# Another written order for all of the attention stage of a hash-attention, mixture and spatial-gating kernel

## The chip, the cores and the metric

The kernel runs on one core of one Trainium2 chip. The metric is the device time of one execution in microseconds (us), the median of three runs. The engines are named as the profile names them: PE is TensorE's matmul, PEld its weight load, DVE is VectorE, ACT is ScalarE, POOL is GpSimd, SP is SyncE, which here only issues DMAs.

## What is computed

Three layers stand one behind the other. The first is attention whose mask is a hash: every query and every key gets six sign bits from a projection, and a query sees the keys with the same bits. The other two are token mixers made of matrix products.

```python
def _attn_ref(q, k, v, proj):            # q, k, v: (2, 8, 768, 64)
    q_bucket, k_bucket = ...             # six sign bits of q @ proj, k @ proj
    mask = q_bucket[:, :, :, None] == k_bucket[:, :, None, :]
    scores = np.where(mask, scale * np.matmul(q, k.transpose(0, 1, 3, 2)), -1000000000.0)
    attn = np.exp(scores - np.max(scores, axis=-1, keepdims=True))
    attn = attn / (np.sum(attn, axis=-1, keepdims=True) + 1e-09)
    return np.matmul(attn, v)

def reference(**kwargs):
    x = attention output, reshaped to (2, 768, 512)
    x = _moe_ref(x)       # k = relu(xk @ w_k); v = k*k @ w_v; r = sigmoid(xr @ w_r); r * v
    return _moe2_ref(x)   # relu(x @ w_in), normalise one half, mix over tokens, gate, @ w_out
```

## The kernel before

**The attention stage.** Two heads form a pair, and there are eight pairs. A pair has two groups (halves of its 768 queries), and a group has six units: two heads times three blocks of 128 queries. So there are 96 units and 16 groups. Nothing decides the order of the work at run time. A table of words in `attention()`, the string `order`, is read word by word, and each word records a few instructions on fixed engines. Each engine then carries out its own instructions in just that order and waits by semaphores for the others. A letter is a step, and the number behind it is the unit, the group, the pair, or the half unit:

- `S` (scores, L395) is four products of 384 columns on PE into one of two score banks of PSUM; the next unit but one needs the same bank again.
- `K` (peak, L405) is DVE's pass over the scores of a unit (scaling, and the row's extreme); it frees the score bank.
- `X` (expo, L417) is the exponential on ACT.
- `T` (group, L427) is three PE transposes of half a unit into one of three PSUM banks. `E` and `V` (evac, L433) copy such a bank into the tile PT: `E` on ACT, `V` on DVE. Every half unit has one of the two, 192 in all.
- `A` (av, L462) is the value products of half a group: six products of 384 columns, which the profile records as twelve matmuls, into one bank, `obank`. Two `A` make a group. `F` (finish, L474) is DVE's multiplication of that bank by the reciprocal sums; the next group's first `A` needs the bank free and so waits for `F`.
- `R` (recip, L442 to L448) is the reciprocal of a group's sums: three short DVE instructions, then four DMAs from SP; `D` (spread) sends the result back as a broadcast that `F` reads.
- `Z` (bits_mm, L293) is the projection of the next pair on PE, eight short matmuls in the profile, into one of the three transpose banks; `G` turns it into signs on DVE (L300) and scales it on POOL (L311). `P` and `B` place these bits by DMA.
- `x`, `v`, `L` are loads; `Q` (L276) splits rows on POOL; `W` with two numbers is step by step the preparation of the first mixer's weights: L42 and L72 on ACT, L45, L50, L56, L63 and L66 on DVE, L77 and L78 on POOL.
- `M`, `N`, `b`, `e`, `p`, `s` are the first work of the next stage (mixing tokens on DVE, ACT and POOL, and gate products of PE), `t` and `Y` set its plan going.

From unit 24 to unit 60 the table repeats itself every 12 units (one pair); before and behind it is irregular.

**The mixers** follow in `mixers()`, whose order comes from a plan of ticks that the change leaves alone. Their matrix products run on PE to the end.

Of the kernel before, what the change touches and what calls it, by code (L numbers as in the profile page):

```python
# [233 lines left out]
def attention(tc, nc, mid, wide, top, dram, ident, msc, omu, misc, cst_sb, pb, epsT, kq, vP, XT, TK0, wr, w_r, wk,
              w_k, w_v, ps_s, ps_t, obank, mix_jobs, r_products, r_sigmoid, tick, now, at_tick, plan_weight, wv, **_):
    PS = bass.MemoryType.PSUM
    with ExitStack() as ctx:
# [340 lines left out]
        order = """
S0 S1 w3 K0 S2 K1 X0 T0 X1 l1 T1 T2 K2 E0 S3 E1 E2 T3 K3 X2 S4 W0.0 Z1 V3 W1.0 X3 T5 K4 T4 E5 X4 G1 S5 T7 E4 T6 E7
K5 S6 T8 S7 K6 X5 T9 R0 E6 E8 X6 T11 S8 V9 Q1.0 T10 T12 K7 Q1.2 E11 T13 S9 Q1.1 E10 W0.1 K8 W0.2 X7 A0 X8 E12 Q1.3  # L580
E13 K9 W0.3 W0.4 Q1.6 D0 T15 T14 T16 E15 X9 S10 P0 Q1.7 E14 Q1.5 K10 S11 E16 T17 K11 W0.5 T18 X10 E18 T19 E19 S12
V17 W1.1 K12 S13 X11 W0.6 T20 E20 P1 T21 v1 A1 T22 Q1.4 E21 T23 S14 X12 W0.7 K13 E22 T25 T24 E23 W1.2 F0 x2 S15 K14
R1 S16 W1.3 X13 K15 T27 X14 A2 E24 L2 W1.4 V25 E27 Z2 W1.6 G2 T29 T28 X15 S17 Q2.3 Q2.2 Q2.0 E29 W1.7 E28 T26 E26
K16 A3 T30 Q2.6 K17 Q2.1 T31 Q2.5 X16 Q2.7 Q2.4 X17 W2.0 E30 S18 E31 T35 K18 T32 T33 V33 S19 E35 E32 T34 X18 S20 T37
K19 T36 B2 E34 X19 E36 K20 S21 T39 V37 K21 S22 V39 T38 V38 X20 X21 T40 E40 S23 T41 E41 T43 T42 E43 K22 D1 S24 W3.0
K23 X22 S25 X23 x3 W0.8 T45 R2 T44 W1.5 F1 A4 A5 R3 W2.1 E44 V45 E42 K24 X24 W2.2 K25 W1.8 L3 W2.3 W3.1 T47 T46 S26
Z3 W2.4 E47 E46 T48 W2.5 W2.6 W2.7 T49 S27 X25 G3 E48 Q3.2 Q3.0 K26 T51 D2 Q3.3 X26 E49 Q3.6 Q3.4 Q3.7 T50 S28 K27
E51 W3.2 S29 F2 X27 W3.3 K28 W3.4 T52 T53 A6 K29 A7 X28 E50 v2 X29 W3.6 E52 W3.7 T54 Q3.5 T55 V53 Q3.1 W4.0 E54 S30
E55 T59 K30 T56 T57 V57 S31 E59 E56 T58 X30 S32 T61 K31 T60 B3 E58 X31 E60 K32 S33 T63 V61 K33 S34 V63 T62 V62 X32
X33 T64 E64 S35 T65 E65 T67 T66 E67 K34 D3 S36 W5.0 K35 X34 S37 X35 x4 W2.8 T69 R4 T68 W3.5 F3 A8 A9 R5 W4.1 E68 V69  # L590
E66 K36 X36 W4.2 K37 W3.8 L4 W4.3 W5.1 T71 T70 S38 Z4 W4.4 E71 E70 T72 W4.5 W4.6 W4.7 T73 S39 X37 G4 E72 Q4.2 Q4.0
K38 T75 D4 Q4.3 X38 E73 Q4.6 Q4.4 Q4.7 T74 S40 K39 E75 W5.2 S41 F4 X39 W5.3 K40 W5.4 T76 T77 A10 K41 A11 X40 E74 v3
X41 W5.6 E76 W5.7 T78 Q4.5 T79 V77 Q4.1 W6.0 E78 S42 E79 T83 K42 T80 T81 V81 S43 E83 E80 T82 X42 S44 T85 K43 T84 B4
E82 X43 E84 K44 S45 T87 V85 K45 S46 V87 T86 V86 X44 X45 T88 E88 S47 T89 E89 T91 T90 E91 K46 D5 S48 W7.0 K47 X46 S49
X47 x5 W4.8 T93 R6 T92 W5.5 F5 A12 A13 R7 W6.1 E92 V93 E90 K48 X48 W6.2 K49 W5.8 L5 W6.3 W7.1 T95 T94 S50 Z5 W6.4
E95 E94 T96 W6.5 W6.6 W6.7 T97 S51 X49 G5 E96 Q5.2 Q5.0 K50 T99 D6 Q5.3 X50 E97 Q5.6 Q5.4 Q5.7 T98 S52 K51 E99 W7.2
S53 F6 X51 W7.3 K52 W7.4 T100 T101 A14 K53 A15 X52 E98 v4 X53 W7.6 E100 W7.7 T102 Q5.5 T103 V101 Q5.1 W8.0 E102 S54
E103 T107 K54 T104 T105 V105 S55 E107 E104 T106 X54 S56 T109 K55 T108 B5 E106 X55 E108 K56 S57 T111 V109 K57 S58
V111 T110 V110 X56 X57 T112 E112 S59 T113 E113 T115 T114 E115 K58 D7 S60 W9.0 K59 X58 S61 X59 x6 W6.8 T117 R8 T116
W7.5 F7 A16 A17 R9 W8.1 E116 V117 E114 K60 X60 W8.2 K61 W7.8 L6 W8.3 W9.1 T119 T118 S62 Z6 W8.4 E119 E118 T120 W8.5  # L600
W8.6 W8.7 T121 S63 X61 G6 E120 Q6.2 Q6.0 K62 T123 D8 Q6.3 X62 E121 Q6.6 Q6.4 Q6.7 T122 S64 K63 E123 W9.2 S65 F8 X63
W9.3 K64 W9.4 T124 T125 A18 K65 A19 X64 E122 v5 X65 W9.6 E124 W9.7 T126 Q6.5 T127 V125 Q6.1 W10.0 S66 B6 E126 E127
K66 T129 E129 T128 E128 S67 x7 W8.8 T131 K67 X66 T130 S68 V131 E130 T133 X67 S69 D9 E133 T132 E132 K68 T135 T134 K69
X68 V135 F9 X69 S70 S71 T137 K70 R10 T136 V136 A20 K71 E134 W10.1 W10.2 E137 T138 X70 T139 X71 L7 E138 T141 S72 E139
S73 M0 D10 E141 T140 T143 R11 E140 K72 X72 T142 K73 S74 E143 M1 K74 Z7 A21 E142 M2 T144 T145 W10.3 G7 S75 W10.4 X73
V144 T146 X74 T147 E145 W11.0 E146 T148 W9.5 K75 S76 S77 T149 X75 V147 Q7.4 K76 E148 T151 X76 E149 K77 Q7.0 T150 X77
F10 Q7.6 S78 V151 S79 D11 Q7.3 K78 T152 T153 V150 v6 E152 A22 A23 X78 T154 V153 W9.8 T155 B7 E155 K79 R12 v7 V154
S80 X79 Q7.1 K80 Q7.2 T157 E157 T156 S81 V156 T158 T159 Q7.7 X80 K81 S82 E158 S83 X81 E159 K82 N0 T161 T160 E161 K83
S84 T163 V160 F11 T162 W10.6 X82 M3 E163 S85 T164 T165 E162 K84 X83 A24 Q7.5 W11.1 X84 A25 W10.5 T166 W10.7 N1 E164
D12 K85 R13 N2 V165 T167 N3 V166 S86 S87 T169 X85 K86 E167 T168 W10.8 E169 T170 F12 X86 S88 E168 T171 A26 K87 K88  # L610
X87 M4 E170 T174 E171 T173 M5 T172 X88 S89 M6 V174 S90 W12.0 T175 K89 E172 E173 K90 N4 N5 X89 W12.1 D13 T177 T176
E177 E176 V175 S91 K91 S92 T178 T179 W11.2 K92 X90 E179 X91 A27 X92 T180 E180 V178 N6 W11.3 T183 S93 M7 R14 S94
W11.4 E183 T182 T181 N7 F13 A28 V182 D14 K93 b0 A29 E181 K94 X93 T184 b1 e0 W11.6 X94 T188 S95 T187 E188 V184 T185
E187 T186 W12.2 b2 W11.5 E186 K95 p0 F14 e1 E185 X95 T190 E190 R15 Y t T189 T191 b3 e2 e3 E191 W11.7 D15 t b4 E189
W12.3 A30 A31 t W11.8 p1 b5 W12.4 W12.6 W12.7 t F15 s0 t s1 t b6
"""
# [573 lines left out]
```

## Time and profile before

| what | value |
|---|---|
| median of three runs | 526.62 us (526.17 to 526.82) |
| the profiled execution | 526.15 us |
| span of its instructions | 524.3 us |
| PE, DVE, ACT, POOL busy in it | 518.0, 417.9, 331.1, 149.3 us |
| evictions L433 on ACT and on DVE | 146 and 46 |

The times in the rows count from the span's start. A row of the timeline has the start, the duration, the engine, the line, the operation, what it writes and reads, sizes and how many instructions were merged into the row; in brackets stands idle time of the engine ahead of it and what ended it. The durations of matmuls are modelled and overlap (a product begins before the one ahead of it is through), so what a block of products costs PE is read as the distance from its start to the start of the next block.

### The profile page before, as it was taken

How to read it: one execution, taken by the hardware profiler on the slowest of the kernel's cores; microseconds unless marked ns; L12 is line 12 of the kernel's file. 1: busy time of each engine (PE TensorE's matmuls, PEld its weight loads, DVE VectorE, ACT ScalarE, POOL GpSimd, SP SyncE). 2: the span in 40 equal slices, each digit the busy share in tenths (PEclk: the TensorE clock that was granted, in tenths of full speed). 3: DMA queues.
4: the chain of work that ended last, by engine and by line, in shares of the span. 5: the costliest groups of instructions: out<-in, count | busy, mean ns of one | idle time of the engine just before them, and what ended most of it. 6: DMA issues, size and time to landing. Idle time of an engine off the chain costs nothing.

```text
span 524.3 us, 8289 instructions
## 1 busy us (share of the span) xinstructions
PE 518.0 (99%) x2850; PEld 417.0 (80%) x2850; DVE 417.9 (80%) x849; ACT 331.1 (63%) x682; POOL 149.3 (28%) x159
## 2 busy tenths in 40 slices
...
GB/s 231 192 210 153 179 191 139 179 170 180 160 164 147 89 71 17 92 5 41 80 41 80 42 67 54 81 40 55 73 126 60 61 45 5 43 7 114 1 20 102
DMA packets 20042, 49.88 MB, mean 95 GB/s; under 512 B 3776, under 2 KB 7424, under 8 KB 20000
## 3 DMA queue, kind: packets, MB, share of 16 engines
...
q10 hardware_dynamic: 432, 0.28, 0.2%
q14 instruction: 19, 0.16, 0.1%
...
## 4 chain that ended last, share of the span: by engine, by line
PE 94%; DVE 4%; ACT 1%; issue 1%; DVEq 0%
PE o L183 13%; PE v L700 12%; PE o L462 12%; PE t L427 11%; PE s L395 11%; PE k L183 9%; PE s L183 7%; PE r L183 6%; PE u L183 5%; PE w L183 5%; DVE p L405 2%; PE z L293 1%; DVE tk L380 1%; DVE rc L442 0%; DVE PT L433 0%
## 5 line engine op out<-in xcount | busy, mean ns | idle before, releaser
L405 DVE TENSOR_SCALAR_CACHE_REDUCE p<-s 128x768 f32<-128x768 f32 x96 | 91.1, 953 | 16.0 <-PE s L395 12.5
L417 ACT ACTIVATE p<-p,m 128x768 f32<-128x768 f32 x96 | 90.1, 940 | 12.9 <-DVE p L405 12.2
L395 PE MATMUL s<-tk 128*128 128x384 f32 x384 | 86.9, 356 | 0.6 <-DVE tk L336 0.4
L131 POOL TENSOR_TENSOR tk<-g,tk 128x384 fp32r<-128x384 f32 x8 | 9.0, 1141 | 270.5 <-PE s L183 233.5
L427 PEld LDWEIGHTS t<-ident,p 128*128 128x128 f32 x576 | 65.8, 140 | 18.6 <-ACT p L417 4.9
L427 PE MATMUL t<-ident,p 128*128 128x128 f32 x576 | 79.8, 275 | 0.2 <-ACT p L417 0.2
L433 ACT COPY PT<-t 128x384 f32<-128x384 f32 x146 | 64.7, 476 | 23.2 <-PE t L427 23.0
L700 PE MATMUL v<-k,wv 128*128 128x512 f32 x288 | 68.8, 389 | 0.0
L462 PE MATMUL o<-PT,v 128*64 128x384 f32 x384 | 66.3, 491 | 0.9 <-DVE XT L474 0.9
L395 PEld LDWEIGHTS s<-tk 128*128 128x128 f32 x384 | 62.6, 189 | 3.2 <-POOL tk L341 0.9
L700 PEld LDWEIGHTS v<-k,wv 128*128 128x128 f32 x288 | 54.1, 188 | 11.2
L276 POOL TENSOR_TENSOR tk<-x,tk 64x384 fp32r<-64x384 f32 x56 | 59.3, 1079 | 10.2 <-DMA tk<-in_kq_dram 9.0
L462 PEld LDWEIGHTS o<-PT,v 128*64 128x64 f32 x384 | 25.8, 136 | 32.1 <-issue 30.4
L686 DVE TENSOR_TENSOR k<-kt,k 128x512 fp32r<-128x512 f32 x24 | 16.6, 690 | 24.8 <-ACT k L685 24.7
L183 PE MATMUL k<-tk,wk 128*128 128x512 f32 x144 | 35.6, 389 | 0.0
L183 PEld LDWEIGHTS k<-tk,wk 128*128 128x128 f32 x144 | 27.0, 188 | 5.6
L130 ACT CAST tk<-g 128x384 fp32r<-128x384 f32 x16 | 8.2, 513 | 36.2 <-DVE g L966 36.2
L156 DVE SCALAR_TENSOR_TENSOR f<-XT,msc,d 128x256 f32<-128x256 f32 x48 | 24.1, 503 | 6.5 <-ACT d L150 5.1
L433 DVE COPY PT<-t 128x384 f32<-128x384 f32 x46 | 24.7, 547 | 2.1 <-PE t L427 2.0
L183 PE MATMUL r<-tk,wr 128*128 128x512 f32 x108 | 25.7, 391 | 0.0
L66 DVE SCALAR_TENSOR_TENSOR w_a<-w_raw,w_p 128x512 f32<-128x512 uint32 x32 | 24.2, 755 | 1.0
L42 ACT ACTIVATE w_a<-w_raw 128x512 f32<-128x512 f32 x32 | 21.7, 678 | 4.7 <-DMA w_raw<-in_w_in_dram 3.7
(188 smaller groups left out, 934.4 us busy)
## 6 DMA issues: line engine op xcount, KB each, us to landing
...
```

The source lines that it names most:

```text
L42: nc.scalar.activation(st["a"].bitcast(F32), st["raw"][:, :, 1].bitcast(F32), AF.Abs)
L66: nc.vector.scalar_tensor_tensor(st["a"].bitcast(F32), st["raw"][:, :, 0], 2.0 ** -52, st["p"].bitcast(F32), op0=ALU.mult, op1=ALU.mult,)
L156: nc.vector.scalar_tensor_tensor(st["f"], x, mu, st["d"], op0=ALU.mult, op1=ALU.add)
L183: nc.tensor.matmul(o, a, x, start=(i == 0), stop=(i == len(seq) - 1))
L276: nc.gpsimd.tensor_sub(tk[l, 1 + 2 * t, o], raw[pp][l, t, o], tk[l, 2 * t, o])
L395: nc.tensor.matmul(s[:, c, :HS], w, t[:, n, c * HS:(c + 1) * HS], start=(n == 0), stop=(n == 1),)
L405: nc.vector.tensor_scalar(c, s[:, :, :HS], -0.125, BIG / 16, op0=ALU.mult, op1=ALU.min, accum_out=m)
L417: nc.scalar.activation(c, c, AF.Exp, bias=m, scale=-1.0, accum_out=den[g][:, u:u + 1])
L427: nc.tensor.transpose(t[:, 128 * n:128 * n + 128], p[:, k0:k0 + 128], ident)
L433: copy(PT[g][:, e, 3 * c:3 * c + 3, 128 * j:128 * j + 128], t[:, :HS].rearrange("p (n q) -> p n q", n=3),)
L462: nc.tensor.matmul(obank[64 * e:64 * e + 64, :HS], vt[g // 2][:, kt, e, :], PT[g][:, e, kt, :], start=(kt == 0), stop=(kt == 5),)
L700: nc.tensor.matmul(o, w, x, start=(c == 0 and k == 0), stop=(c == 7 and k == 2))
```

## The change

It replaces the string `order` and nothing else. Both strings hold 1004 words, and each engine does the same kinds of work. 61 half units are evicted by DVE (`V`) in the new string and 131 by ACT, where it was 46 and 146. The value products stand in 19 uninterrupted runs instead of 20, and six of the seven projections `Z` stand directly ahead of or behind a run of value products, where it was two.

```diff
-X47 x5 W4.8 T93 R6 T92 W5.5 F5 A12 A13 R7 W6.1 E92 V93 E90 K48 X48 W6.2 K49 W5.8 L5 W6.3 W7.1 T95 T94 S50 Z5 W6.4
...
+W5.5 K47 S48 V89 S49 F5 T92 D6 T93 W6.1 W5.8 E92 V93 A12 X47 W7.1 K48 L5 A13 K49 W6.2 W6.3 R7 W7.2 E90 Z5 W6.4 W7.3
```

**PE at the head of a pair, before** (units 36 to 38; `z` is the projection, `o` the value products, `t` transposes, `s` scores):

```order
L395 MATMUL s<-tk_0_84 128x384 x8
L427 MATMUL t<-ident,p 128x128 x6
L462 MATMUL o_76<-PT,v 64x384 x12
L427 MATMUL t<-ident,p 128x128 x6
L395 MATMUL s<-tk_0_84 128x384 x4
L293 MATMUL z<-x,msc 32x384 x4
L427 MATMUL t<-ident,p 128x128 x6
L395 MATMUL s<-tk_1_85 128x384 x4
```

The same place on PE with the change:

```order
L395 MATMUL s<-tk_0_84 128x384 x8
L427 MATMUL t<-ident,p 128x128 x6
L462 MATMUL o_76<-PT,v 64x384 x12
L293 MATMUL z<-x,msc 32x384 x4
L427 MATMUL t<-ident,p 128x128 x3
L395 MATMUL s<-tk_0_84 128x384 x4
L427 MATMUL t<-ident,p 128x128 x6
```

The projection moved from between scores and transposes to directly behind the value products.

**DVE from the end of one pair to the head of the next, before** (`p` is the pass over the scores, `rc` the reciprocal, `XT` the finish, `PT` an eviction):

```order
L405 TENSOR_SCALAR p,m<-s 128x768 x2
L442 TENSOR_SCALAR rc_95<-den 128x6
L443 RECIPROCAL rc_95<-rc_95 128x6
L445 STREAM_TRANSPOSE rt<-rc_95 128x32
L474 TENSOR_TENSOR XT<-o_76,rb 128x384
L442 TENSOR_SCALAR rc_96<-den 128x6
L443 RECIPROCAL rc_96<-rc_96 128x6
L445 STREAM_TRANSPOSE rt<-rc_96 128x32
L433 COPY PT<-t 128x3x128
L405 TENSOR_SCALAR p,m<-s 128x768
```

The same place on DVE with the change:

```order
L405 TENSOR_SCALAR p,m<-s 128x768
L442 TENSOR_SCALAR rc_95<-den 128x6
L443 RECIPROCAL rc_95<-rc_95 128x6
L445 STREAM_TRANSPOSE rt<-rc_95 128x32
L405 TENSOR_SCALAR p,m<-s 128x768 x2
L433 COPY PT<-t 128x3x128
L474 TENSOR_TENSOR XT<-o_76,rb 128x384
L433 COPY PT<-t 128x3x128
L405 TENSOR_SCALAR p,m<-s 128x768 x2
```

The first reciprocal moved from directly ahead of the finish to two score passes and one eviction ahead of it; the second moved behind (it is six rows further on). An eviction now stands ahead of the finish and another behind it.

## Rows read from the trace of the kernel before

**Rows 1.** The page: busy time, share of the span, instructions of three engines.

```profile
PE 518.0 (99%) x2850; PEld 417.0 (80%) x2850; DVE 417.9 (80%) x849; ACT 331.1 (63%) x682; POOL 149.3 (28%) x159
```

**Rows 2.** The page: the chain that ended last, by engine.

```profile
PE 94%; DVE 4%; ACT 1%; issue 1%; DVEq 0%
```

**Rows 3.** Waits of PE, 16 to 222 us: total us, times, longest.

```profile
PE o L462 <- DVE XT L474: 0.9, 2, 0.5
```

**Rows 4.** Timeline of PE, about a projection between scores and transposes.

```profile
110.14 0.94 PE L395 MATMUL s<-tk 128*128 128x384 f32 x4
111.01 0.85 PE L293 MATMUL z<-x,msc 128*32 128x384 f32 x8
111.79 0.87 PE L427 MATMUL t<-ident,p 128*128 128x128 f32 x6
112.42 0.94 PE L395 MATMUL s<-tk 128*128 128x384 f32 x4
113.21 0.82 PE L427 MATMUL t<-ident,p 128*128 128x128 f32 x6
113.78 1.70 PE L395 MATMUL s<-tk 128*128 128x384 f32 x8
```

**Rows 5.** Timeline of PE, a projection that directly follows value products.

```profile
37.27 0.85 PE L293 MATMUL z<-x,msc 128*32 128x384 f32 x8
38.05 0.87 PE L427 MATMUL t<-ident,p 128*128 128x128 f32 x6
```

**Rows 6.** Timeline of PE, a short and a long run of value products.

```profile
198.81 2.16 PE L462 MATMUL o<-PT,v 128*64 128x384 f32 x12
200.90 0.88 PE L427 MATMUL t<-ident,p 128*128 128x128 f32 x6
201.53 1.66 PE L395 MATMUL s<-tk 128*128 128x384 f32 x8
203.03 0.82 PE L427 MATMUL t<-ident,p 128*128 128x128 f32 x6
203.77 4.09 PE L462 MATMUL o<-PT,v 128*64 128x384 f32 x24
207.79 0.88 PE L427 MATMUL t<-ident,p 128*128 128x128 f32 x6
```

**Rows 7.** Timeline of all engines, the first of the two waits of PE.

```profile
51.24 1.31 POOL L78 TENSOR_TENSOR wr<-w_b,w_a 128x512 fp32r<-128x512 f32 x1
...
51.38 1.20 DVE L442 TENSOR_SCALAR rc<-den 128x6 f32<-128x6 f32 x1
...
52.97 0.52 DVE L474 TENSOR_TENSOR XT<-o,rb 128x384 f32<-128x384 f32 x1
...
53.54 0.87 PE L462 MATMUL o<-PT,v 128*64 128x384 f32 x4 [0.39 <-DVE XT L474]
```

**Rows 8.** One line's instructions: duration in ns, shortest, median, longest.

```profile
L442 DVE TENSOR_SCALAR rc<-den x16: 159/170/1265, 18.4 to 212.8; 128x6 f32<-128x6 f32 x16
```

**Rows 9.** Timeline, one unit from its scores to its second transposes.

```profile
44.28 0.94 PE L395 MATMUL s<-tk 128*128 128x384 f32 x4
...
45.35 0.96 DVE L405 TENSOR_SCALAR_CACHE_REDUCE p<-s 128x768 f32<-128x768 f32 x1 [0.23 <-PE s L395]
...
46.34 0.94 ACT L417 ACTIVATE p<-p,m 128x768 f32<-128x768 f32 x1 [0.28 <-DVE p L405]
...
47.44 0.54 PE L427 MATMUL t<-ident,p 128*128 128x128 f32 x3
```

**Rows 10.** Windows of one pair each: length, then busy us of PE, PEld, DVE, ACT, POOL.

```profile
50.00:76.00 26.00, 25.61 (x177) 18.90 (x176) 24.49 (x50) 20.95 (x47) 20.84 (x20) 1.00 0.79 197
76.00:102.00 26.00, 26.00 (x181) 19.29 (x180) 22.48 (x50) 21.57 (x47) 15.90 (x17) 1.00 0.67 150
```

**Rows 11.** Timeline of DVE: two evictions and the pass behind them.

```profile
126.74 1.02 DVE L433 COPY PT<-t 128x384 f32<-128x384 f32 x2
127.68 0.95 DVE L405 TENSOR_SCALAR_CACHE_REDUCE p<-s 128x768 f32<-128x768 f32 x1
```

More of the change, by code (lines that the diff above doesn't have):

```diff
@@ L578, in attention @@
         order = """
[L579 to L593, printed above, removed]
@@ L594, in attention @@
-E82 X43 E84 K44 S45 T87 V85 K45 S46 V87 T86 V86 X44 X45 T88 E88 S47 T89 E89 T91 T90 E91 K46 D5 S48 W7.0 K47 X46 S49
-X47 x5 W4.8 T93 R6 T92 W5.5 F5 A12 A13 R7 W6.1 E92 V93 E90 K48 X48 W6.2 K49 W5.8 L5 W6.3 W7.1 T95 T94 S50 Z5 W6.4
-E95 E94 T96 W6.5 W6.6 W6.7 T97 S51 X49 G5 E96 Q5.2 Q5.0 K50 T99 D6 Q5.3 X50 E97 Q5.6 Q5.4 Q5.7 T98 S52 K51 E99 W7.2
-S53 F6 X51 W7.3 K52 W7.4 T100 T101 A14 K53 A15 X52 E98 v4 X53 W7.6 E100 W7.7 T102 Q5.5 T103 V101 Q5.1 W8.0 E102 S54
-E103 T107 K54 T104 T105 V105 S55 E107 E104 T106 X54 S56 T109 K55 T108 B5 E106 X55 E108 K56 S57 T111 V109 K57 S58
@@ L599, in attention @@
[L599 to L613, printed above, removed]
@@ L614, in attention @@
-E187 T186 W12.2 b2 W11.5 E186 K95 p0 F14 e1 E185 X95 T190 E190 R15 Y t T189 T191 b3 e2 e3 E191 W11.7 D15 t b4 E189
-W12.3 A30 A31 t W11.8 p1 b5 W12.4 W12.6 W12.7 t F15 s0 t s1 t b6
+S0 S1 w3 K0 S2 K1 X0 T0 l1 X1 T1 T2 K2 E0 S3 E1 V2 K3 T3 X2 E3 S4 W0.0 Z1 K4 T5 G1 S5 T4 X3 T7 X4 W1.0 E4 T6 E7 V5
+S6 E6 K5 K6 P0 X5 T9 T8 S7 E9 v1 T10 T11 X6 S8 V8 R0 Q1.2 T12 K7 Q1.1 E10 W0.1 E11 T13 X7 K8 W0.2 S9 E12 W1.1 S10 X8
+T14 E13 T15 K9 V14 X9 K10 W0.3 Q1.3 P1 E15 A0 T16 T19 E16 X10 T17 E17 S11 Q1.0 V19 S12 T18 T20 K11 K12 Q1.4 T21 X11
@@ new lines, in attention @@
+E18 E20 Q1.6 S13 S14 X12 Q1.7 T23 T22 W0.4 E22 E21 K13 K14 X13 W0.6 A1 R1 E23 T25 T27 Q1.5 W1.2 W1.3 T24 E25 W0.7
+S15 X14 V27 S16 E24 T26 T28 T29 K15 x2 D0 L2 V26 X15 K16 F0 S17 Z2 G2 W1.4 Q2.3 V28 W1.6 Q2.0 K17 W1.7 X16 A2 Q2.1
+Q2.2 V29 A3 W0.5 T31 Q2.5 T30 Q2.6 Q2.7 X17 Q2.4 W2.0 E31 S18 T32 V30 T33 E32 K18 E33 S19 X18 T34 T35 S20 K19 E34 B2
+V35 X19 T37 T36 S21 E37 K20 W3.0 T39 V36 X20 D1 T38 K21 R2 E39 x3 E38 X21 S22 T40 K22 E40 W0.8 T41 S23 T43 E43 X22
+T42 W1.5 K23 S24 V41 S25 F1 T44 D2 T45 W2.1 W1.8 E44 V45 A4 X23 W3.1 K24 L3 A5 K25 W2.2 W2.3 R3 W3.2 E42 Z3 W2.4
@@ new lines, in attention @@
+W3.3 X24 T47 S26 G3 W2.5 Q3.3 T46 T49 X25 W2.6 E47 v2 S27 Q3.1 T48 E49 V46 Q3.5 K26 X26 E48 T51 T50 K27 S28 F2 Q3.7
+E50 V51 S29 Q3.0 T52 Q3.4 T53 Q3.2 W2.7 Q3.6 A6 W3.4 V52 X27 A7 K28 X28 W3.6 E53 K29 T55 W3.7 X29 T54 W4.0 E55 S30
+T56 V54 T57 E56 K30 E57 S31 X30 T58 T59 S32 K31 E58 B3 V59 X31 T61 T60 S33 E61 K32 W5.0 T63 V60 X32 D3 T62 K33 R4
+E63 x4 E62 X33 S34 T64 K34 E64 W2.8 T65 S35 T67 E67 X34 T66 W3.5 K35 S36 V65 S37 F3 T68 D4 T69 W4.1 W3.8 E68 V69 A8
+X35 W5.1 K36 L4 A9 K37 W4.2 W4.3 R5 W5.2 E66 Z4 W4.4 W5.3 X36 T71 S38 G4 W4.5 Q4.3 T70 T73 X37 W4.6 E71 v3 S39 Q4.1
@@ new lines, in attention @@
+T72 E73 V70 Q4.5 K38 X38 E72 T75 T74 K39 S40 F4 Q4.7 E74 V75 S41 Q4.0 T76 Q4.4 T77 Q4.2 W4.7 Q4.6 A10 W5.4 V76 X39
+A11 K40 X40 W5.6 E77 K41 T79 W5.7 X41 T78 W6.0 E79 S42 T80 V78 T81 E80 K42 E81 S43 X42 T82 T83 S44 K43 E82 B4 V83
+X43 T85 T84 S45 E85 K44 W7.0 T87 V84 X44 D5 T86 K45 R6 E87 x5 E86 X45 S46 T88 K46 E88 W4.8 T89 S47 T91 E91 X46 T90
+W5.5 K47 S48 V89 S49 F5 T92 D6 T93 W6.1 W5.8 E92 V93 A12 X47 W7.1 K48 L5 A13 K49 W6.2 W6.3 R7 W7.2 E90 Z5 W6.4 W7.3
+X48 T95 S50 G5 W6.5 Q5.3 T94 T97 X49 W6.6 E95 v4 S51 Q5.1 T96 E97 V94 Q5.5 K50 X50 E96 T99 T98 K51 S52 F6 Q5.7 E98
@@ new lines, in attention @@
+V99 S53 Q5.0 T100 Q5.4 T101 Q5.2 W6.7 Q5.6 A14 W7.4 V100 X51 A15 K52 X52 W7.6 E101 K53 T103 W7.7 X53 T102 W8.0 E103
+S54 T104 V102 T105 E104 K54 E105 S55 X54 T106 T107 S56 K55 E106 B5 V107 X55 T109 T108 S57 E109 K56 W9.0 T111 V108
+X56 D7 T110 K57 R8 E111 x6 E110 X57 S58 T112 K58 E112 W6.8 T113 S59 T115 E115 X58 T114 W7.5 K59 S60 V113 S61 F7 T116
+D8 T117 W8.1 W7.8 E116 V117 A16 X59 W9.1 K60 L6 A17 K61 W8.2 W8.3 R9 W9.2 E114 Z6 W8.4 W9.3 X60 T119 S62 G6 W8.5
+Q6.3 T118 T121 X61 W8.6 E119 v5 S63 Q6.1 T120 E121 V118 Q6.5 K62 X62 E120 T123 T122 K63 S64 F8 Q6.7 E122 V123 S65
@@ new lines, in attention @@
+Q6.0 T124 Q6.4 T125 Q6.2 W8.7 Q6.6 A18 W9.4 V124 X63 A19 K64 X64 W9.6 E125 K65 T127 W9.7 X65 T126 W10.0 B6 D9 V127
+S66 T128 W8.8 E128 V126 T129 E129 K66 S67 R10 T130 K67 T131 X66 S68 T132 E130 X67 K68 T133 S69 S70 V133 E131 E132
+X68 T134 K69 E134 X69 T135 S71 E135 W11.0 K70 x7 T136 W9.5 F9 T137 S72 L7 X70 V136 T139 T138 A20 K71 A21 E137 X71
+W10.1 V138 T140 V139 T141 K72 W10.2 E140 v6 T142 E141 R11 M0 W10.3 S73 D10 T143 X72 S74 M1 K73 E142 V143 Q7.2 K74
+F10 T144 T145 S75 Z7 X73 X74 E144 E145 W10.4 K75 G7 W10.5 W9.8 X75 M2 A22 T146 T147 S76 E147 T151 E151 V146 T149 K76
```

9 lines of the change are left out of this document (added).

## Prediction

> **What bounds the kernel now.** I read the page's first part first: PE is busy 518.0 us of the span, DVE 417.9 and ACT 331.1 [rows 1]. Then the chain that ended last: 94% of it is PE [rows 2]. A busy PE can still hide waits, so the third view is PE's own list of waits inside the attention stage. From 16 to 222 us it has one line: value products that waited for DVE's finish, twice, 0.9 us in all [rows 3]. So PE paces the attention stage almost without a gap. A new order can win in two ways only: PE's own products become cheaper by their neighbours, or these 0.9 us go. It can lose in one way: PE waits where it did not. That 15 evictions go from ACT to DVE wins nothing by itself, since nobody waited for ACT; it spends DVE's slack.
>
> **PE's own time: the projections.** The cost of a block is the distance between the starts of blocks. A projection between scores and transposes takes 0.78 us (111.01 to 111.79). But its neighbours pay too: the four score products ahead of it last 0.87 (110.14 to 111.01), where ahead of transposes they last 0.79 (112.42 to 113.21), and the six transposes behind it 0.63 (111.79 to 112.42) instead of 0.57 (113.21 to 113.78) [rows 4]. That is 0.08 + 0.06 = 0.14 us. Directly behind value products a projection takes 0.78 as well (37.27 to 38.05) [rows 5], and the value products' own neighbours have paid already [rows 6]. So each of the four projections more that stand beside value products saves 0.14: 4 x 0.14 = 0.56 us.
>
> **PE's own time: one run less.** A run of 12 recorded products takes 2.09 us (198.81 to 200.90), one of 24 takes 4.02 (203.77 to 207.79) [rows 6]; two short ones are 4.18, so joining saves 0.16. The transposes ahead of a run take 0.74 (203.03 to 203.77) instead of 0.57, of which the scores get 0.08 back that they pay behind transposes: in a double block of scores (1.50 us, 201.53 to 203.03) the second four cost 0.71 instead of 0.79 [rows 4, 6]. The transposes behind a run take 0.63 instead of 0.57. So one run less saves 0.16 + 0.09 + 0.06 = 0.31, and both edits 0.87 us. This needs no free engine and no luck. I take it whole.
>
> **The waits for the finish.** At 51.38 us the first instruction of a reciprocal takes 1.20 us; it ends as POOL's addition (51.24, 1.31 long) ends [rows 7]. The same instruction has a median of 0.17 us over its 16 places, and 1.27 at its longest [rows 8]. The reciprocal stands directly ahead of the finish in DVE's queue, so the finish starts only at 52.97, and the value products at 53.54, after 0.39 us of idle PE [rows 7]. The Trainium skill explains this kind of row (SBUF — State Buffer, "Who interferes with whom"): some DVE instructions need the port pair that GpSimd also uses, and whichever comes second blocks until the other is through. By the same section an instruction with a PSUM source, as these evictions are, does not take part; no row here shows the reverse.
>
> In the new order that reciprocal stands two score passes and one eviction earlier, the other one stands behind the finish, and the finish is recorded before the transposes that precede the value products. What is late next on DVE is then an eviction and two passes, with their own slack (below). So I count the 0.9 us [rows 3] as gone.
>
> **What the new order adds: work for DVE.** Two evictions in a row and the next pass start 0.94 us apart [rows 11], 0.47 each. Fifteen more are 7 us of DVE over the stage; in each repeated pair it is 8 evictions instead of 6, so 0.94 us. They lie beside PE's work as long as DVE has room. DVE was busy 24.49 of 26 us in one pair and 22.48 in the next, with 50 instructions in both [rows 10]; the 2.0 us between them is what blocked instructions cost. After the change that would be 25.4 and 23.4. There is room, but little in a pair with blocked instructions. ACT gets lighter, which is worth nothing here.
>
> **What it adds: the reciprocal among the passes.** The chain of a unit is in one place of the trace without company: scores start at 44.28, the pass at 45.35 (1.07 later), the exponential at 46.34, the transposes at 47.44 [rows 9]. At the end of a pair the new order alternates four scores and six transposes (0.79 + 0.57 = 1.36 us). Scores of unit i+2 need the bank of unit i, so the pass has 2 x 1.36 = 2.72 us from the start of its scores, and needs 1.07 + 0.96 = 2.03: 0.69 to spare. The transposes of unit i come 2 x 1.36 + 0.79 = 3.51 behind the scores and need 3.16: 0.35 to spare. Into this the reciprocal is now put, between two passes. Its whole length on DVE is 1.59 us where its first instruction was blocked (51.38 to 52.97) [rows 7], so 0.56 unblocked. The pass ahead of it ends 2.03 behind its own scores, the reciprocal 2.59, that is 1.23 behind the scores of the next unit: its pass is 0.16 late, which the spare time covers. Blocked by another 1.1, it is 1.26 late, and PE waits 1.26 - 0.69 = 0.57 us. Four pairs end so: between 0 and 2.3 us. POOL is busy 15.90 to 20.84 of 26 us [rows 10], so the instruction often meets one; but it then waits for the rest of it, on average half of 1.3 us, which the spare time nearly covers. I take 0.15 a pair, 0.6 us in all, nearer to the lower end since that is what the slack of the rows gives.
>
> Elsewhere (the irregular first 24 and last 36 units) I found passes with the same 2.72 us or less between scores that share a bank, as before, and cost the difference at nothing, with 0.5 us to either side for the range. At the very end a gate product moves ahead of the last value products; the mixing steps on DVE behind the last finish become fewer, so I cost it at nothing too. The same loads stand in the order, and PE waits for none of them inside the stage [rows 3].
>
> **Sum.** 526.15 (the profiled execution) - 0.87 - 0.9 + 0.6 = 524.98. The median of the runs lies 0.47 above that execution, so 525.45, stated as 525.4.
>
> **Rivals.**
> - *The waits come back elsewhere.* The port conflict is not removed, only put ahead of other work. If in two to four pairs the reciprocal is fully blocked, PE loses 1.1 to 2.3 us in place of 0.6. For it: POOL does the same work as before. Against it: in the trace only two blocked instructions reached PE at all [rows 3], although the difference of the two pairs is 2.0 us each [rows 10]. Time: 526.62 - 1.77 + 1.1 to 2.3 = 526.0 to 527.2.
> - *DVE becomes the bound, slower.* With 0.94 us more a pair it needs 25.4 of 26 us in a pair with blocked instructions. From one blocked instruction more (1.1 us) it no longer fits: 26.5, so 0.5 us a pair; with two more, 1.6 a pair. Over four pairs 2.0 to 6.4 us, so 526.8 to 531.2, in the middle 529. For it: rows 10 and the spare 0.35 us ahead of transposes. Against it: an eviction has no strict due time except through three banks, and the other pairs had 3.5 us idle. The Trainium skill speaks on this side (Perfetto Trace Analysis, "Optimizing Scalar/DVE Operations"): where DVE is saturated, work goes from it to Scalar, and the change moves it the other way. By the page the sum would come out in this rival; by the busy share of 80% [rows 1] DVE isn't saturated.
> - *The order does not do what it says.* Excluded for PE: the order of the built program shows the projections beside the value products.
>
> **How the numbers follow.** The forecast (new waits between 0 and 0.9, so 524.3 with 0.5 gained elsewhere, to 525.9) gets 0.52, the returning waits 0.36, the DVE bound 0.12. A measurement of this kernel can tell about 0.2%, 1.05 us, from no change; that puts the line for faster at 525.57. Of the forecast 0.46 lies below it, and 0.02 of the second case if the start also gains: 0.48 faster, 0.40 within, 0.12 slower. The range goes from 524.3, nothing new and 0.4 gained, to 527.4, all four reciprocals blocked and 0.3 lost elsewhere; some 0.07 is left out below and 0.13 above.
>
> **What would show it.** Right: projections with 0.78 us behind value products and no 0.87 ahead of them; 19 runs, the long ones 4.02; no wait of PE for the finish; the next stage's products starting 1 to 1.5 us earlier than before. Wrong: scores waiting for the pass (PE for DVE L405) more than 1 us in all, with a long L442 ahead; transposes waiting for ACT or for a bank; DVE above 25 us in 26. The forecast falls if these sum to more than 1.8 us.

## The result, and the profile after

The change is slower: 531.28 us (529.70 to 533.40, six runs) against 526.00 (525.58 to 526.82, six runs) of the kernel before in the same comparison, a ratio of 1.0096 with an interval of 1.0071 to 1.0121. The profiled execution took 530.67 us with a span of 528.0, where before it was 526.15 and 524.3. So 3.7 us of its loss lie inside the span, and some 0.8 us around it.

The page after: busy time (as [rows 1]), then the chain that ended last (as [rows 2]).

```profile
PE 518.5 (98%) x2850; PEld 417.6 (79%) x2850; DVE 422.7 (80%) x864; ACT 325.1 (62%) x667; POOL 150.2 (28%) x159
...
PE 88%; DMA 4%; DVE 3%; ACT 2%; POOL 2%; issue 1%; SPq 1%; POOLq 0%; DVEq 0%; ACTq 0%
```

PE is as busy as before. But the chain has 88% of PE where it had 94%, and 4% of DMA where it had none. PE's list of waits says where the time is; it is the view of [rows 3], same stretch, total us, times, longest:

```profile
PE o L462 <- DVE XT L474: 3.6, 3, 2.5
PE s L395 <- DVE p L405: 0.7, 1, 0.7
PE t L427 <- DVE zb L300: 0.4, 1, 0.4
```

That is 4.7 us of waits instead of 0.9. The line that was to go, value products waiting for the finish, has grown from 0.9 to 3.6. The third line lies at the start of the stage:

```profile
16.33 0.92 PE L427 MATMUL t<-ident,p 128*128 128x128 f32 x6 [0.38 <-DVE zb L300]
```

Transposes wait there for DVE's sign step of a projection (L300).

**The finish waits for its broadcast.** Timeline of the longest wait, rows of DVE, PE and of SP's queue (SPq):

```profile
160.31 1.29 SPq L448 DMA_DIRECT2D ds<-rt  x4
161.71 1.09 SPq L455 DMA_DIRECT2D rb<-ds  x2
...
167.78 0.56 DVE L474 TENSOR_TENSOR XT<-o,rb 128x384 f32<-128x384 f32 x1 [2.58 <-DMA rb<-ds]
...
168.39 2.16 PE L462 MATMUL o<-PT,v 128*64 128x384 f32 x12 [2.47 <-DVE XT L474]
```

The same broadcast and finish in the kernel before:

```profile
162.08 1.20 SPq L455 DMA_DIRECT2D rb<-ds  x2
...
168.62 0.55 DVE L474 TENSOR_TENSOR XT<-o,rb 128x384 f32<-128x384 f32 x1
```

DVE stood idle for 2.58 us ahead of the finish `F10` until a DMA, the broadcast `rb<-ds` of the reciprocal sums (`D10`), had landed. In SP's queue that broadcast stands behind the four DMAs of the twelfth reciprocal `R11`, whose DVE part is done only at 160.3. The table of before has `D10` ahead of `R11`; the new one has it behind. The broadcast isn't issued later than before (161.71 against 162.08). But the new order wants it earlier: DVE was ready for `F10` at 165.20, where before the finish came at 168.62, 3.1 us after the broadcast was complete (165.55 in the trace).

At two ends of pairs the finish waits in the same way. SP's queue of the change there, then the chain of work, then the same place of the queue before:

```profile
122.51 0.44 SPq L38 DMA_DIRECT2D w_raw<-in_w_k_dram  x1
123.00 1.15 SPq L455 DMA_DIRECT2D rb<-ds  x2
```
```profile
123.54 7.32 DMA rb<-ds
130.86 0.02 issue
130.88 0.57 DVE XT L474
```
```profile
122.59 1.13 SPq L455 DMA_DIRECT2D rb<-ds  x2
123.83 0.51 SPq L38 DMA_DIRECT2D w_raw<-in_w_k_dram  x1
```

A weight load of 512 KB (`W9.0`) now stands ahead of the broadcast (two DMAs of 96 KB), where it stood behind it. By the traces the broadcast was complete 7.9 us after its issue (123.00 to 130.86), before 3.4 us (122.59 to 125.96). Its second DMA took 7.32 us to land and the value products lost 0.68 us: 1.42 from the transposes' start at 130.08 to theirs at 131.50, where transposes ahead of value products take 0.74 [rows 6].

**A reciprocal among the passes was blocked.** DVE, and the scores of PE behind it:

```profile
148.68 1.50 DVE L442 TENSOR_SCALAR rc<-den 128x6 f32<-128x6 f32 x1
```
```profile
150.08 0.82 PE L427 MATMUL t<-ident,p 128*128 128x128 f32 x6
151.55 1.84 PE L395 MATMUL s<-tk 128*128 128x384 f32 x8 [0.65 <-DVE p L405]
```

From 150.08 to 151.55 are 1.47 us for transposes that cost 0.57 [rows 4]: 0.90 lost, and the double block of scores behind takes 0.18 more than in [rows 6]. The blocked instruction ends as POOL's L77 (148.86, 1.29 long) ends. It is longer than that one because it already met the tail of the POOL instruction ahead (L276, 147.89 to 148.91). It belongs to `R10`, which lies behind unit 60, where the table no longer repeats. At the ends of the four repeated pairs (`R2`, `R4`, `R6`, `R8`) the same instruction took 0.39, 0.32, 0.17 and 0.69 us, and PE waited for no pass there.

**PE's own products did become cheaper.** Timeline of PE:

```profile
131.50 4.09 PE L462 MATMUL o<-PT,v 128*64 128x384 f32 x24 [0.60 <-DVE XT L474]
135.52 0.85 PE L293 MATMUL z<-x,msc 128*32 128x384 f32 x8
136.30 0.55 PE L427 MATMUL t<-ident,p 128*128 128x128 f32 x3
...
137.97 0.94 PE L395 MATMUL s<-tk 128*128 128x384 f32 x4
138.75 1.14 PE L427 MATMUL t<-ident,p 128*128 128x128 f32 x9
```

The long run costs 4.02 (131.50 to 135.52), the projection behind it 0.78, and the scores 0.78, as [rows 4 to 6] price them. With such prices put on every block of the stage, its blocks sum to 0.95 us less than before (an estimate), and the time over the prices grows by 4.65: the difference is the 3.7 us of the span.

### The profile page after: what moved, and what is told of

Read it like the earlier page. It is cut to its first block, busy times and chain, and to the rows that moved or that the text cites. A ratio compares the mean times of both kernels' runs of the same rounds, so it can differ in the third digit from the quotient of the medians.

```text
span 528.0 us, 8278 instructions
## 1 busy us (share of the span) xinstructions
PE 518.5 (98%) x2850; PEld 417.6 (79%) x2850; DVE 422.7 (80%) x864; ACT 325.1 (62%) x667; POOL 150.2 (28%) x159
## 3 DMA queue, kind: packets, MB, share of 16 engines
HBM read 45.11 MB, written 3.19 MB: 91 GB/s over the span
## 4 chain that ended last, share of the span: by engine, by line
PE 88%; DMA 4%; DVE 3%; ACT 2%; POOL 2%; issue 1%; SPq 1%; POOLq 0%; DVEq 0%; ACTq 0%
PE o L183 13%; PE v L700 12%; PE o L462 11%; PE k L183 9%; PE t L427 9%; PE s L395 8%; PE s L183 7%; PE r L183 6%; PE u L183 5%; PE w L183 5%; DMA rb<-ds 4%; PE z L293 1%; ACT p L417 1%; DVE p L405 1%; POOL tk L336 1%
## 5 line engine op out<-in xcount | busy, mean ns | idle before, releaser
L427 PE MATMUL t<-ident,p 128*128 128x128 f32 x576 | 80.2, 275 | 0.6 <-DVE zb L300 0.4
L427 PEld LDWEIGHTS t<-ident,p 128*128 128x128 f32 x576 | 66.5, 140 | 16.6 <-issue 7.3
L433 ACT COPY PT<-t 128x384 f32<-128x384 f32 x131 | 58.9, 473 | 16.1 <-PE t L427 15.8
L276 POOL TENSOR_TENSOR tk<-x,tk 64x384 fp32r<-64x384 f32 x56 | 59.9, 1084 | 12.0 <-DMA tk<-in_kq_dram 10.0
L433 DVE COPY PT<-t 128x384 f32<-128x384 f32 x61 | 33.4, 551 | 7.8 <-PE t L427 7.8
L56 DVE SCALAR_TENSOR_TENSOR w_b<-w_raw,w_a 128x512 uint32<-128x512 uint32 x32 | 23.6, 738 | 0.7
```

Of the source, the lines that this page charges most:

```text
L56: nc.vector.scalar_tensor_tensor(st["b"], st["raw"][:, :, 1], 0xC0000000, st["a"], op0=ALU.bitwise_and, op1=ALU.bitwise_or,)
L276: nc.gpsimd.tensor_sub(tk[l, 1 + 2 * t, o], raw[pp][l, t, o], tk[l, 2 * t, o])
L427: nc.tensor.transpose(t[:, 128 * n:128 * n + 128], p[:, k0:k0 + 128], ident)
L433: copy(PT[g][:, e, 3 * c:3 * c + 3, 128 * j:128 * j + 128], t[:, :HS].rearrange("p (n q) -> p n q", n=3),)
```

## The experiments

Each diff is of the table of words, cut to the words that move; where several places change alike, it shows the first of them. The theory at first: broadcasts come late by what stands ahead of them in SP's queue (A). The rivals: DVE is too full (B), and what each expectation names. "Before" is always the kernel before on the same chip in the same comparison; it had a median between 525.76 and 526.35.

**One cause each, and both.** `e1_spread_ahead` moves `D10`, `e2_loads_behind` the four weight loads, `e3_both` both.

```diff
-E141 R11 M0 W10.3 S73 D10 T143
+E141 D10 R11 M0 W10.3 S73 T143
```
```diff
-K20 W3.0 T39 V36 X20 D1 T38
+K20 T39 V36 X20 D1 W3.0 T38
```

> The changed order with one word moved: D10 (the broadcast of group 10's sums) stands ahead of R11 instead of two scores behind it, so that its DMA no longer stands behind R11's four DMAs in SP's queue. Theory A (the broadcast lands late): the finish of group 10, which waited 2.58 us for the broadcast, waits 0 to 0.3, and the time falls by about 2.5 us, to 528.8. Theory B (DVE is the bound, because of 15 more evictions): PE then waits for a score pass or a bank instead; less than 0.5 us comes back.

> The changed order with four weight loads (W3.0, W5.0, W7.0, W9.0; 512 KB each) recorded directly behind the broadcasts D1, D3, D5, D7 instead of directly or shortly ahead of them, as in the kernel before. Theory A: the broadcast takes less than the 7.3 us seen behind a load, the two waits of the value products at 78 and 130 us (0.60 and 0.68 us beyond the block's usual time) go, 1.2 us less, 530.0. Theory B: no change beyond 0.3 us.

> Both of the edits to the changed order. Theory A: 3.7 us less than the changed kernel, 527.5; PE waits for no finish. What is left over the kernel before must then be a blocked reciprocal among the score passes (0.9 us at 150 us) and the start (0.5 us at 15 us), less 0.9 us of cheaper products. Theory B: 531, with waits for passes and banks.

Measured, here and below as median, ratio to the kernel before and its interval: 530.30 (1.0090, 1.0061 to 1.0119); 530.89 (1.0102, 1.0079 to 1.0126); 526.92 (1.0024, 1.0004 to 1.0043). Alone they bring next to nothing, together more than 4 us. The queue's order is the main cause, but the two places don't add up. A part of that is PE's clock, which can fall behind a long wait (below): three of the four runs of `e2_loads_behind` show a mean granted clock of 0.994 to 0.997, nine of the ten of `e3_both` 0.999 or 1.000. With `D10` ahead the finish is still waited for three times, 2.5 us in all, the longest (1.8) at the end of a pair; with the loads behind, the one wait at `F10` stays:

```profile
PE o L462 <- DVE XT L474: 2.6, 1, 2.6
PE s L395 <- DVE p L405: 0.8, 1, 0.8
PE t L427 <- DVE zb L300: 0.4, 1, 0.4
```

**The same loads ahead in the old order.** `e4_before_loads_ahead` puts the four loads ahead of the broadcasts in the kernel before.

```diff
-E43 K22 D1 S24 W3.0 K23
+E43 K22 W3.0 D1 S24 K23
```

> The kernel before with one thing of the change alone: the same four weight loads recorded directly ahead of the broadcasts D1, D3, D5, D7. Theory A: the broadcast lands late in the kernel before too; its finish stands 6 to 8 us behind the issue there, so PE loses 0 to 0.7 us at each of four places, 0.5 to 2 us in all, 526.5 to 528. Theory B: no change, since DVE's load is the same.

Measured: 526.65 (1.0000, 0.9964 to 1.0035). There is no loss in the median, but two of ten runs lay at 529.7 and 530.3. The first of these is the profiled one, and in it PE waited 3.5 us for the finish: DVE stood idle for the broadcast 1.31 us at 105.93, behind a load that had moved ahead, and 2.48 us at 118.82, where none had. So in the old order a load ahead costs nothing in most runs. The room is small in both orders. At the last three of these places the kernel before has 6.7 to 7.5 us from the issue of a broadcast until its finish is ready to run, and the change 5.7 to 6.8. With a load ahead the broadcast took 4.8 to 7.9 us to complete, with the load behind it 3.4 to 3.7 in the kernel before. That the old order stands it by these tenths is my reading.

**The change once more, to see its spread.**

> The changed kernel as it is, on the chip of the next three runs, for a comparison on one chip. Expected 1.010 of the kernel before, spans from 527.5 to 530.

Measured: 532.47 (530.34 to 533.49, four runs; 1.0113, 1.0084 to 1.0142). Its profiled run waited 4.7 us for the finish, four times. Rows of PE, and windows with the granted clock (the third number from the end) behind the longest wait:

```profile
169.94 3.25 PE L462 MATMUL o<-PT,v 128*64 128x384 f32 x12 [2.82 <-DVE XT L474]
173.13 1.41 PE L427 MATMUL t<-ident,p 128*128 128x128 f32 x6
174.29 0.94 PE L395 MATMUL s<-tk 128*128 128x384 f32 x4
```
```profile
168.00:170.00 2.00, 0.06 (x2) 0.06 (x3) 0.67 (x2) 0.26 (x1) 0.00 (x0) 1.00 0.02 8
170.00:172.00 2.00, 2.00 (x10) 0.91 (x12) 2.00 (x5) 1.23 (x2) 0.00 (x0) 0.71 0.16 57
172.00:174.00 2.00, 2.00 (x8) 0.88 (x5) 0.88 (x2) 0.42 (x2) 1.94 (x2) 0.50 0.13 46
```

After 2.82 us without work the granted clock fell to 0.50, the lower of its two levels. The run of twelve value products took 3.19 us instead of 2.09 [rows 6] and the transposes 1.16 instead of 0.63: 1.6 us on top of the wait. In the profile of the change shown first, the wait of 2.47 us had no such fall behind it. The length of the wait alone doesn't decide this, as the same place shows in `e2_loads_behind` and in `e12_spread_earlier` (below):

```profile
168.03 2.16 PE L462 MATMUL o<-PT,v 128*64 128x384 f32 x12 [2.62 <-DVE XT L474]
```
```profile
166.06 3.06 PE L462 MATMUL o<-PT,v 128*64 128x384 f32 x12 [2.55 <-DVE XT L474]
```

Behind 2.62 us the clock stayed at 1.00, behind 2.55 it was 0.50 from 168 to 170 us. Such falls are a part of why the runs of the change lie 529.7 to 533.4: its slowest shows a mean clock of 0.997, the others 1.000.

**Other repairs that were tried.** `e6_reciprocal_behind` takes the reciprocals away from the passes; `e7_before_projection_moved` puts only the projections of the change into the old order; `e8_evictions_back` gives 15 evictions back to ACT.

```diff
-K21 R2 E39 x3
...
-S25 F1 T44
+K21 E39 x3
...
+S25 F1 R2 T44
```
```diff
-F1 A4 A5 R3 W2.1
...
-S26 Z3 W2.4 E47
...
-S27 X25 G3 E48
+F1 A4 A5 Z3 R3 W2.1
...
+S26 W2.4 G3 E47
...
+S27 X25 E48
```
```diff
-K32 T63 V60 X32 D3
+K32 T63 E60 X32 D3
```

> The changed order with D10 ahead of R11 and the four weight loads behind their broadcasts, and besides R2, R4, R6, R8 moved from between two score passes to directly behind the finish F1, F3, F5, F7. Theory A (a reciprocal blocked by POOL makes a pass late, the scores wait): the 1.06 us that transposes and scores lost at 148 us go, and the time falls by 1.0 us against the same order with the reciprocals where the change has them, to 525.9 where that one has 526.9. Theory B (passes are late since DVE has 15 evictions more): the wait stays or turns up at another pass, 0 to 0.3 us less.

> The kernel before with one part of the change alone: four projections (Z3 to Z6) stand directly behind the value products instead of between scores and transposes, and their sign steps G3 to G6 three weight steps earlier. By the sum of the prediction 4 x 0.14 = 0.56 us less: in the trace no score block of 0.87 us ahead of a projection in these four places. A rival: the bank of the projection is held longer, and a transpose waits for the sign step, 0.3 us at each place, which gives it back.

> The changed order with D10 and the four loads mended, and besides 15 of the 61 evictions of VectorE given to ScalarE, 46 as before, two in each repeated pair and seven elsewhere. Theory A: the evictions hide beside PE's work on either engine, within 0.5 us of the same order with 61 (526.9). Theory B (DVE too full): 1 us or more less than that, and no wait of the scores for a pass.

Measured: 537.56 (1.0226, 1.0194 to 1.0259), 526.51 (1.0035, 1.0004 to 1.0067) and 528.54 (1.0046, 1.0024 to 1.0068).

The first is a clear miss: 10.6 us above `e3_both`. It moved `R2`, `R4`, `R6` and `R8`, but the reciprocal whose block reached PE is `R10`, which stands where it stood. The wait for the pass is gone all the same, since in the shifted time `R10` was not blocked (0.16 us at 158.60); so this run doesn't test theory A, and `e9_no_addition` below does. The reciprocal heads the path reciprocal, DMA, broadcast, finish, and moving the four later made everything behind them late: 5.2 us of waits for the finish, 4.7 for evictions, and a mean clock of 0.992 to 0.997 in all four runs. The second shows no gain from the projections alone. Transposes behind the scores that lost their projection now wait for their unit's exponential on ACT, as PE's weight loads show:

```profile
61.63 0.51 PEld L427 LDWEIGHTS t<-ident,p 128*128 128x128 f32 x4 [0.33 <-ACT p L417]
```

At 60.67 the scores take 0.96 to the next block instead of 0.79, and so at four places: 0.7 us against the 0.56 to be gained. The third speaks against rival B: with DVE lighter the kernel gained nothing. Its ratio is 0.0022 (some 1.2 us) above that of `e3_both`, with intervals that overlap. In its profiled run, the slowest of six (530.90), transposes waited 1.4 us for ACT's evictions.

**The blocked addition by itself.** L442 adds 1e-9 and is the instruction that blocks. The row sums hold the largest element's exponential, which is 1, and in this precision the addition does not change them. `e9_no_addition` is `e3_both` without it, `e10_before_no_addition` the kernel before without it.

```diff
-            nc.vector.tensor_scalar_add(rc[:, 0:6], den.pop(g), 1e-9)
-            nc.vector.reciprocal(rc[:, 0:6], rc[:, 0:6])
+            sums = den.pop(g)
+            nc.vector.reciprocal(rc[:, 0:6], sums)
```

> The change with the four weight loads behind the broadcasts and the eleventh broadcast ahead of the twelfth reciprocal (as in e3_both), and one thing more: the addition of 1e-9 to the softmax sums on VectorE (L442) is left out of the kernel, and the reciprocal is taken straight from the sums. In e3_both one of the four reciprocals among the score passes had its addition blocked and PE stood 1.06 us (148.41). Theory A (the blocked addition makes the score pass late): no line of scores waiting for p of 0.5 us or more, and 1.0 to 1.3 us less than e3_both, so about 525.8. Rival B (the pass is late because VectorE's queue is full there): the wait stays, with 0.17 less, and the time is 526.7 to 526.9.

> The kernel before with the same addition of 1e-9 left out, its order untouched. This measures by itself the term of the prediction that counted 0.9 us of waits for the finish. Theory A (those two waits were made by the blocked addition): they go, and the time is 0.8 to 1.0 us below before, 525.0 to 525.3. Rival B (without that addition the finish is held up by the next blocked instruction, or by the broadcast): the waits stay at 0.5 us or more, time within 0.3 of before.

Measured: 526.30 (1.0003, 0.9972 to 1.0033) and 525.11 (0.9984, 0.9953 to 1.0014; ten of eleven runs from 524.90 to 525.80, before 525.76). In the old order PE's list of waits is now empty: what the prediction said of these two waits was right. In the new order the wait for the pass is gone, but 0.9 us of it came back at `F10`, where there had been 0.2:

```profile
PE o L462 <- DVE XT L474: 0.9, 1, 0.9
```

**The start, and the eleventh broadcast earlier still** (both without the addition).

```diff
-T5 G1 S5 T4 X3
+T5 G1 T4 S5 X3
```
```diff
-F9 T137 S72
...
-E141 D10 R11
+F9 D10 T137 S72
...
+E141 R11
```

> e9_no_addition with the sixth block of scores put behind the fifth block of transposes at the start, where it stands in the kernel before. Theory A (this one swap made the wait of 0.63 us near 15.4): the wait near 15.4 is 0.2 us or less and the time 0.4 to 0.5 below e9_no_addition. Rival B (the start is set by when the first loads land): the stall only moves by a block and the time stays within 0.1.

> e11_start_as_before with the eleventh broadcast put directly behind the tenth finish, some 6 us earlier in SP's queue. Theory A (what is left of the wait of the eleventh value products, 0.27 us in e3_both, is still the broadcast): 0.2 to 0.3 us below e11_start_as_before, no wait for the finish of 0.1 us or more near 163. Rival B (that rest is the finish itself behind VectorE's other work): no change. With all four edits the written order without its waits should be 1.0 to 1.6 us below the kernel before if the cheaper products of the prediction (0.87 us) are real and kept.

Measured: 527.27 (1.0026, 0.9999 to 1.0054) and 525.66 (0.9992, 0.9967 to 1.0018). Both miss. The stall at the start only moved by a block (0.53 us instead of 0.65). In the second the word moved, but the issue hardly did: 153.27 after 153.45, since it waits in both for the finish `F9` to free its tile. Its profiled run, the slowest of eleven (529.16), waited 2.6 us at `F10`: the broadcast landed at 165.4. Its median lies 1.6 us lower, with intervals that overlap, and I can't say by what.

**What holds the eleventh broadcast.** Two loads of SP's queue (`W11.0`, 512 KB, and `v6`, 384 KB) stand ahead of it in the new order and behind it in the old; and POOL issues 2.3 MB of loads (one of 768 KB, four of 384) from 150 us on. `e13_loads_behind_tenth` is `e3_both` with `D10` behind `F9` and the two loads behind `F10`; `e14_x_behind_too` moves the word `x7` as well; `e15_tenth_alone` is the change with the repair at `F10` only; `e16_all` is `e13_loads_behind_tenth` without the addition.

```diff
-E135 W11.0 K70 x7 T136 W9.5 F9 T137
...
-E140 v6 T142 E141 D10 R11
...
-F10 T144
+E135 K70 x7 T136 W9.5 F9 D10 T137
...
+E140 T142 E141 R11
...
+F10 v6 W11.0 T144
```

> e3_both with the eleventh broadcast directly behind the tenth finish, and the weight load (512 KB) and the load of values (384 KB) of SP's queue put behind the eleventh value products, as they stand in the kernel before. Theory A (the broadcast runs behind these two loads in one queue): it lands by 158 us, the wait of the eleventh value products is gone in every run, the time is 0.3 to 0.6 us below e3_both (526.9) and its runs lie closer together: median 526.2 to 526.6, no run with a fallen clock. Rival B (POOL's 768 KB load of the same time holds the broadcast up): it still lands at 161 us or later, and waits of up to 2.8 us stay in some runs.

> e13_loads_behind_tenth with the 768 KB load on POOL put behind the broadcast in the written order as well. Theory A: nothing further is gained by it, and since the last pairs' additions on POOL need that load, PE may wait for them: between 0 and 1.5 us slower than e13_loads_behind_tenth. Rival B: only here is the wait for the broadcast gone, 0.3 to 0.6 us below e13_loads_behind_tenth.

> The change as it is, with the repair at this one place only (eleventh broadcast directly behind the tenth finish, the two loads behind the eleventh value products); the loads ahead of the broadcasts of the four pairs stay. Theory A: the place costs the change its 2.5 us and, in the runs where the clock falls behind that wait, some 2 us more, so 2.5 to 4 us below the change: 527.5 to 529, with what is left in the waits at the ends of the pairs. Rival C (the wait only moves on to the next pair's end, as it did when the broadcast alone was moved): 530 to 531.

> e13_loads_behind_tenth with the addition of 1e-9 to the softmax sums (L442) left out. All losses that the traces of the change name are then repaired but the wait of 0.65 us at the start. Theory A: the cheaper products (0.9 us) and the two waits of before (0.9 us) are then left as gains against 0.65 us lost at the start: 524.5 to 525.2. Rival D (something else of the change costs time that no wait shows): 525.8 or more.

Measured: 526.28 (0.9997, 0.9982 to 1.0011), 526.72 (0.9999), 528.61 (1.0046, 1.0026 to 1.0067) and 525.98 (0.9995, 0.9980 to 1.0009). With the loads behind, all eleven runs of the first lie within 1.4 us and the clock fell in none. But the broadcast was complete only at 163.91, not by 158: in landing, rival B was right. The wait is gone because the finish itself came at 164.21. `e15_tenth_alone` prices this one place at some 2.7 us of the change's 5.3 (531.28 less 528.61), though its runs spread from 526.7 to 534.6. `e14_x_behind_too` tested nothing: POOL issued its load at 149.93 and the broadcast came at 154.14 all the same, since it waits for the finish `F9` to free its one tile. In `e16_all` the wait is back:

```profile
162.20 0.85 PE L293 MATMUL z<-x,msc 128*32 128x384 f32 x8
164.30 2.16 PE L462 MATMUL o<-PT,v 128*64 128x384 f32 x12 [1.25 <-DVE XT L474]
```

The finish `F10` starts at nearly one time in `e3_both` (163.99), `e9_no_addition` (163.64) and `e16_all` (163.69), however early PE gets there, and later still in the two kernels ahead (164.55 and 165.45). That speaks for POOL's loads: what is gained ahead of this place is waited away at it. The DMA packets bear it out. In `e13_loads_behind_tenth` no load stood ahead of the broadcast in SP's queue; it was issued at 154.85, yet its first packet started at 159.99, while packets of POOL's loads ran from 152 to 162.5. In the kernel before it was issued at 162.08, as those loads ended, and was complete 3.5 us later. That this is why the repairs did not add up is my reading.

**A place of its own for that broadcast**, issued without waiting for `F9`, in an unused end of the tile of `x7`; and the old order beside it, both without the addition.

```diff
-            R[g] = at.tile([128, 3, 128], F32, tag="rb", name="rb")
+            if g == 10:
+                R[g] = spare[7].rearrange("p (n q) -> p n q", n=3)
+            else:
+                R[g] = at.tile([128, 3, 128], F32, tag="rb", name="rb")
```

> e16_all (addition of 1e-9 left out as there) with the eleventh broadcast written to an unused end of the tile that the last pair's 768 KB load fills, so that it waits for no finish, and put directly behind that load in the written order. Theory A (the broadcast came behind POOL's 2.3 MB of loads because its one buffer held it back until the tenth finish): it is issued near 150 us, lands by 156, and the wait of the eleventh value products is gone in every run: 0.5 to 1.3 us below e16_all (525.98), so 524.7 to 525.5, and its runs lie within 1 us but for a few. Rival B (these loads hold it up wherever it is issued): it lands at 160 us or later and the time is e16_all's.

> The kernel before with the addition of 1e-9 left out, again (e10_before_no_addition, 525.11), beside e17_own_place. Both orders are then without their named waits but for 0.65 us at the start of the new one (0.17 in the old). Theory A (the cheaper products are real): e17_own_place is 0.3 to 0.6 us below this kernel (0.87 less 0.48 at the start), near this measurement's limit. Rival (they are given back in places no wait shows): e17_own_place is level with it or above.

Measured: 524.89 (524.53 to 526.18; 0.9979, 0.9967 to 0.9991) and 525.10 (0.9978, 0.9962 to 0.9994). SP's queue, and all that is left of PE's list of waits from 16 to 222 us (L457, L426 and L299 are L455, L427 and L300 of the other kernels):

```profile
151.82 1.11 SPq L457 DMA_DIRECT2D x<-ds  x2
```
```profile
PE t L426 <- DVE zb L299: 0.4, 1, 0.4
```

The wait is gone: the finish `F10` starts at 162.40 and finds its broadcast there. So the time is as theory A of this pair says, but not the way there: the issue came 2 us later than expected, only 1.0 us earlier than in `e16_all`, and the broadcast was complete at 161.77 (163.59 in `e16_all`), not by 156. That fits POOL's loads all the same: two of the five were issued ahead of it here (150.51 and 151.30), four in `e16_all` (150.21 to 152.27). The old order runs with nothing on that list at all. Both kernels beat the one before. Between the two orders 0.2 us are left in the medians and 0.3 in the spans (522.9 and 523.2), less than the 0.3 to 0.6 expected and below what this measurement can tell apart.

## Why the prediction was wrong

- *PE's own time: right by the prices.* 0.87 us expected, 0.95 by the prices of the blocks. It isn't shown in the time: with the named waits repaired, the new order leads the old by 0.2 to 0.3 us, after 0.48 lost at the start, and that isn't clear of noise. `e7_before_projection_moved` gave the gain of its projections back in waits.
- *The waits for the finish, 0.9 us counted as gone: the step that failed.* It asked what is late next on DVE, and found only an eviction and two passes. A finish also reads the broadcast, and that comes through SP's queue. "The same loads stand in the order, and PE waits for none of them" took the loads' number for their order. The table shows `W3.0` to `W9.0` now ahead of `D1` to `D7`, `W11.0` and `v6` ahead of `D10`, and `D10` behind `R11`; none was costed. The step's own mechanism held in the old order: without the blocked addition both waits went (`e10_before_no_addition`, `e18_before_no_addition_again`). But in place of 0.9 us came 3.6 in the profiled run, 3.8 by the starts of the blocks, and more where the clock fell. With the queue mended in `e3_both`, 4.4 of the 5.3 us came back. The signs of being wrong that the prediction listed would not have found this: scores waited 0.7 us for a pass, and DVE stayed below 25 us in 26. Only its sign of being right, no wait of PE for the finish, did.
- *The reciprocal among the passes: right in mechanism, wrong in place and size.* The four pairs that were put at 0.6 us cost nothing. The block that reached PE came at `R10`, in the part where the difference was put at nothing. There it cost 0.90 us and 0.18 behind it, where 0.57 was the bound for a full block. The blocked instruction was longer (1.50 us against 1.27 [rows 8]): the prediction let it wait for the rest of one POOL instruction, half of 1.3 us on average, but here it met the end of one and all of the next. That the sum, 1.1 us, lies inside the 0 to 2.3 foreseen for the four pairs is luck. The row agrees with the Trainium skill (SBUF — State Buffer, "Who interferes with whom") in that the instruction was held until POOL's ended. By the recorded starts, though, it came 0.18 us ahead of L77 and still let it go first.
- *Start and end at nothing: off by 0.48 us.* At 15.46 the transposes take 0.65 us over their price, where before the nearest such stall is 0.17; 0.38 of it is the wait for the sign step shown above. Swapping two words back did not cure it.
- *Rivals.* By number the nearest is DVE as the bound, 526.8 to 531.2, but only by luck, for its mechanism falls: DVE was busy 23.0 to 23.6 us in every 26 from 50 to 154, where a pair with blocked instructions was put at 25.4, and taking evictions off it gained nothing. So the advice of the Trainium skill (Perfetto Trace Analysis, "Optimizing Scalar/DVE Operations") had no saturated DVE to work on here. "The waits come back elsewhere", 526.0 to 527.2, was nearest in kind, but it put them in the port conflict and not in a queue.
- *The range* (524.3 to 527.4) was built of PE's products, reciprocals on DVE and 0.3 to 0.4 us elsewhere. No DMA was a term of it.

Open: why some 0.3 to 1.0 us more lie around the span in the change, what else is in the 0.65 us at the start, and whether the broadcast waits for POOL's loads in the DMA engines or in the memory behind them.
